# Fourteen weight pieces in turn behind the last transpose, and zero products counted by product time, in a one-core transformer block

## The chip, the core and the metric

The kernel runs on one core of a Trainium2 chip. The core has a matrix engine (PE, with its weight loads shown apart as PEld), a vector engine (DVE), a scalar engine (ACT), a general engine (POOL) and a sync engine (SP) that issues nearly all transfers. Every engine works through its own instruction queue strictly in order; engines wait for one another by semaphores. The metric is device time in microseconds (us), the median of several runs; lower is better.

## The reference, cut to what matters

One pre-norm transformer block on 2048 tokens of width 640: attention with 32 query heads of width 20 that share one key head and one value head, then a gated MLP of inner width 1536.

```python
n = layernorm(x)
q, k, v = n @ wq, n @ wk, n @ wv          # k and v have one head, q has 32
p = softmax(q k^T * 20 ** -0.5)           # every query sees all 2048 keys
h = x + (p @ v, heads side by side) @ wo
m = layernorm(h)
out = h + (gelu(m @ w_gate) * (m @ w_up)) @ w_down
```

## The kernel before

**Tiles and units.** The 2048 rows are 16 tiles of 128. Queries go in chunks of two tiles (the last two chunks have one). A unit is two groups of four heads for both tiles of a chunk (four groups where the chunk has one tile), which makes 512 columns in each of four row strips; a unit meets all 16 key tiles. One step, a unit with one key tile, is a *QK group*: four matmuls of 512 columns (L1149) that fill four score banks in PSUM. There are 512 QK groups in all. Scores are exponentiated either on ACT (L1489, into `pa`) or on DVE by an integer trick (L1583, into `pd`, copy 0); copies 1 and 2 of `pd` are copy 0 plus a constant, added on POOL (L1552, function `add_both`, both copies at once; L1538, one copy) or on DVE (L1532). *PV groups* (L1228) multiply `v_ext` with `pa` or `pd` into an accumulator bank. `v_ext` holds V times three factors; L604 makes the two scaled versions on POOL, 18 small instructions in the first 54 us.

**The head.** Each x tile is loaded, gets its statistics (L426), waits for a power on POOL (L446), is normed on DVE (L496, into `xn_tmp`) and transposed into `xn1T`: tiles 0 and 1 on PE, the other 14 by transposing transfers on SP (L487). When both tiles of a pair are in `xn1T`, a key/value job on PE (L548, reading `xn1T` and `wk`) makes their keys and values, copied out at L618 or L617. QK groups of the pair can follow only then.

**A finished unit.** Its accumulator is copied to `osb` on DVE (L1255), transposed by SP into `onr` (L725), and divided by its sums: a reciprocal on DVE (L679, waits for the transpose) and a product on POOL (L693). When a chunk is complete its rows are transposed (L754), multiplied with `wo`, normed again, and run through the MLP between the QK and PV groups of later chunks.

**What sets the order.** A planner in the kernel's Python builds all five queues before anything runs. It holds a modelled clock for each engine, takes the engine that is free first, and lets that engine's decision function commit the next instruction. Costs in the planner are constants: a QK or PV group 216 ns, a change between them 105 ns more (`pe_sw`), `add_both` 1010 ns, L604 100 ns for two tiles. Queues on the chip are then fixed in that order, whatever the chip's times turn out to be. So a changed cost or a moved transfer changes the order of later instructions all over the program.

**Weights.** Four loads on SP (L983) bring `wo` (800 KB), `wg`, `wu` and `wd` (1920 KB each). They may be planned once SP's modelled clock is past 30 us, with a lower priority than any transpose that is ready then.

**Zero products.** The clock of PE is granted by the chip and falls to half in some stretches. When PE has nothing else that fits, `fill` (L1352) adds a group of four matmuls with a zero weight into an open accumulator; the result is unchanged. `quiet` permits this when PE's planned busy time, changes of mode included, was under `QUIET` = 0.5 of the last 3400 ns. `fill` also asks that the unit has more than 8 products to come, and that the keys of tiles 0 to 3 are there.

Of the kernel before, what the change touches and what calls it, by code (L numbers as in the profile page):

```python
# [19 lines left out]


class _Op:
    __slots__ = ("eng", "fn", "deps", "t0", "end", "vis", "idx", "dma", "need", "count", "sem", "clock")

    def __init__(self, eng, fn, deps, t0, end, vis, dma):
        self.eng = eng
        self.fn = fn
        self.deps = deps
        self.t0 = t0
        self.end = end  # L30
        self.vis = vis
        self.dma = dma
        self.need = False
        self.count = 0
        self.sem = None
        self.clock = None


class _Plan:
# [60 lines left out]
    def resolve(self):  # L100


        pos = {e: 0 for e in self.ENGINES}
        known = {e: ({f: -1 for f in self.ENGINES}, set()) for e in self.ENGINES}
        self.waits = {e: [] for e in self.ENGINES}
        left = sum(len(v) for v in self.ops.values())
        while left:
            moved = False
            for e in self.ENGINES:
                while pos[e] < len(self.ops[e]):  # L110
                    op = self.ops[e][pos[e]]
                    if any(d.clock is None for d in op.deps):
                        break
                    kn, kd = known[e]
                    need = []
                    for d in sorted(op.deps, key=lambda o: -o.idx):
                        if (d in kd) if d.dma else (kn[d.eng] >= d.idx):
                            continue
                        need.append(d)
                        ck, cd = d.clock  # L120
                        for f in self.ENGINES:
                            kn[f] = max(kn[f], ck[f])
                        kd |= cd
                    best = {}
                    dmas = []
                    for d in need:
                        if d.dma:
                            dmas.append(d)
                        elif d.idx > best.get(d.eng, (-1, None))[0]:
                            best[d.eng] = (d.idx, d)  # L130

                    ws = sorted(dmas + [v[1] for v in best.values()], key=lambda d: d.vis)
                    for d in ws:
                        d.need = True
                    self.waits[e].append(ws)
                    ck = dict(kn)
                    cd = set(kd)
                    if op.dma:
                        cd.add(op)
                    else:  # L140
                        ck[e] = op.idx
                    op.clock = (ck, cd)
                    pos[e] += 1
                    left -= 1
                    moved = True
            assert moved, "the plan has a cycle"
        for e in self.ENGINES:
            n = 0
            for op in self.ops[e]:
                if op.need and not op.dma:  # L150
                    n += 1
                    op.count = n

    def emit(self, name, eng, sems):
        done = 0
        for op, waits in zip(self.ops[name], self.waits[name]):
            for d in waits:
                if d.dma:
                    eng.wait_ge(d.sem, 16)
                else:  # L160
                    eng.wait_ge(sems[d.eng], d.count)
            ins = op.fn(eng)
            if op.dma:
                ins.then_inc(op.sem, 16)
            elif op.need:
                ins.then_inc(sems[name], 1)
                done += 1
                assert done == op.count
# [36 lines left out]
def bass_sequential_preLN__grouped_kv_mqa__glu_gated_geglu__prompt_kernel(  # L205
# [126 lines left out]
        return n / 0.96 + 67.0  # L332

    POOL_ADD = 580.0
    POOL_ADD2 = 1010.0
    SP2 = 1
    SP2D = (450.0, 450.0, 450.0)
    SP2P = (3, 3, 3)
    SP2G = (300.0, 300.0, 300.0)
    ADD_MIN = 1  # L340
    PVF = 99
    QUIET = 0.5
    PADD_DVE = 1
    PADD_LEN = (3, 3, 3)
    PRA = 3
# [9 lines left out]
    LOCKW = 200.0  # L355
    YIELD = 500.0
    WQA = 1
    ADDW = 100.0
    MISCMAX = 1500.0
    L_PE, L_ACT, L_DVE, L_POOL = 232.0, 310.0, 150.0, 100.0  # L360
# [211 lines left out]
    def kv_job(tiles):  # L572
# [24 lines left out]
        def vthen(b):  # L597
            nt = len(tiles)
            vi = ps[:, b * 512:b * 512 + 32 * nt].rearrange("p (t e) -> p t e", t=nt)[:, :, 0:Dh]

            def vfin(op):
                free_bank(b)
                for w in (1, 2):
                    task(("pool",), (lambda w: lambda e: e.tensor_scalar(  # L604
                        v_ext[:, t0:t0 + nt, w, 0:Dh], v_ext[:, t0:t0 + nt, 0, 0:Dh], CH_W[w], None, ALU.mult))(w),
                        60 + 20 * nt, L_POOL, [("v", t, 0) for t in tiles] + [("vone", w)],
                        [("v", t, w) for t in tiles], 0)

            flex_copy(v_ext[:, t0:t0 + nt, 0, 0:Dh], vi, 20 * nt, [("b", b), ("vone", 0)],
                      [("v", t, 0) for t in tiles], 0.5, vfin)  # L610
# [157 lines left out]
    def wo_job(t, s, h):  # L768
        pieces = []
        for c in range(NC_D):  # L770
            pieces.append((mm(lambda b: bank(b, HALF), onT[:, s, c, :], wo_sb[:, c, h * HALF:(h + 1) * HALF],
                              c == 0, c == NC_D - 1), c_mm(HALF), [("onT", s), "wo"]))

        def then(b):
            if h == 1:
# [43 lines left out]
    def gu_pieces(w, b, fc):  # L819
        n = len(BATCHES[b]) * P  # L820
        x0 = xcol[BATCHES[b][0]]
        res = []
        for i in range(per_job(b)):
            f = fc + i
            for c in range(NC_D):
                res.append((mm((lambda i: lambda bk: ps[:, bk * 512 + i * n:bk * 512 + (i + 1) * n])(i),
                               w[:, c, f * P:(f + 1) * P], xn2T[:, c, x0:x0 + n], c == 0, c == NC_D - 1), c_mm(n),
                            [("xn2T", xcol[t]) for t in BATCHES[b]] + ["wg" if w is wg_sb else "wu"]))
        return res

    def gview(b, fc, k):
# [76 lines left out]
    def down_job(b, t, h):  # L908
        c0 = BATCH_COL[b] + (t - BATCHES[b][0]) * P
        pieces = [(mm(lambda bk: bank(bk, HALF), gbuf[:, fc, c0:c0 + P], wd_sb[:, fc, h * HALF:(h + 1) * HALF],  # L910
                      fc == 0, fc == NFC - 1), c_mm(HALF), [("g", fc, c0 // P), "wd"]) for fc in range(NFC)]

        def then(bk):
            down_left[b] -= 1
# [64 lines left out]
    for w in (1, 2):  # L979
        ptask((lambda w: lambda e: e.memset(shifts[:, w - 1:w], CH_SHIFT[w] * 65537))(w), 40, [],  # L980
              [("sh", w)], 1.5)
    for nm, o, v in (("wo", wo_sb, A_wo), ("wg", wg_sb, B_w_gate), ("wu", wu_sb, B_w_up), ("wd", wd_sb, B_w_down)):
        sp_tasks.append(_Task(("sp",), (lambda o, v: lambda e: e.dma_start(o[:], cview(v)))(o, v), 1500, 12000,  # L983
                              [], [nm], 9.0, None, lambda: plan.free["sp"] > 30000.0))

    def pe_sw(t, mode):

# [344 lines left out]
        return False  # L1332

    def quiet(t):
        busy = 0.0
        for o in reversed(plan.ops["pe"]):
            if o.end < t - 3400.0:
                break
            busy += min(o.end, t) - max(o.t0, t - 3400.0)
        return busy < QUIET * 3400.0  # L1340

    def fill(t):

        u = next((u for u in open_units() if u["acc"] is not None and all(u["started"]) and u["todo"] > 8), None)
        if u is None or not all(("k", k) in plan.w and plan.ready("pe", [("k", k)], ()) <= t for k in range(4)):
            return False
        ab = u["acc"]

        def fn(e):
            ins = None  # L1350
            for r in range(4):
                ins = e.matmul(ps[32 * r:32 * r + 32, ab * 512:(ab + 1) * 512], zz[:], kT4[:, 0:512], start=False,  # L1352
                               stop=False, tile_position=(0, 32 * r))
            return ins
        sw = pe_sw(t, "v")
        state["mode"] = "v"
        plan.commit("pe", fn, 216.0 + sw, L_PE, ["zz"] + [("k", k) for k in range(4)], [("b", ab)], at=t)
        state["fills"] = state.get("fills", 0) + 1
        return True

# [182 lines left out]

    def add_both(t):

        x = pend[1].pop(0)
        y = pend[2].pop(0)
        s = x["slot"]
        h = slice(s * 256, (s + 1) * 256)

        def fn(e):
            return e.tensor_tensor(pd32[:, 1:3, h], pd32[:, 0, h].unsqueeze(1).to_broadcast([P, 2, 256]),  # L1552
                                   shifts[:].unsqueeze(2).to_broadcast([P, 2, 256]), ALU.add)
        op = plan.commit("pool", fn, POOL_ADD2, L_POOL, [("pd", 0, s), ("sh", 1), ("sh", 2)],
                         [("pd", 1, s), ("pd", 2, s)], at=t)
        x["add"](1, op)
        y["add"](2, op)

    def dve_decide(t):
        imm = 1e12  # L1560
# [176 lines left out]
        return s  # L1737

    sems = {e: sem("c_" + e) for e in plan.ENGINES}
    n = 0  # L1740
    for e in plan.ENGINES:
        for op in plan.ops[e]:
            if op.dma:
                op.sem = sem("d%d" % n)
                n += 1
    outs = [op for op in plan.ops["sp"] if op.dma]

    with nc.Block() as block:

        @block.sync  # L1750
        def _(e):
            plan.emit("sp", e, sems)
            for op in outs[-NT:]:
                e.wait_ge(op.sem, 16)

        @block.scalar
        def _(e):
# [46 lines left out]
```

## Time and profile before

| | us |
|---|---|
| median of 5 runs | 793.57 |
| lowest and highest of them | 790.85, 795.47 |
| the profiled execution | 790.85 |
| span of the profiled execution, first to last instruction | 789.0 |
| ACT busy | 730.5 (93%) |
| PE busy (weight loads apart) | 694.2 (88%) |
| POOL busy | 655.6 (83%) |
| DVE busy | 614.0 (78%) |
| mean granted clock of PE | 0.984 |

The profile's page sums the whole program. Views of the trace go closer: the timeline lists instructions by start, with the idle time before each and what ended it; the chain follows the work that ended last back to its cause; a view by stretches gives for each one the busy time of an engine, the number of instructions in brackets, the granted PE clock, the busy share of the 16 transfer engines and the GB/s that they moved. "Issue to landing" is the time from the start of a transfer's instruction to the semaphore of its end. The program's zero products are 148 matmuls, so 37 groups.

### The profile page before, as it was taken

The numbers are of one execution on the slowest core, as the hardware profiler recorded it, in microseconds if no ns is written. First come the engines' busy times: TensorE is split into PE (matmuls) and PEld (weight loads), VectorE is DVE, ScalarE is ACT, GpSimd is POOL, SyncE is SP. The second block draws the span as 40 slices with busy tenths as digits, with TensorE's granted clock in tenths as the row PEclk, the third lists the DMA queues.
The fourth block names the chain that finished last, engine by engine and source line by source line (L and its number), as shares of the span: only waits on it lengthen the run. The fifth ranks groups of instructions, "written<-read, shape, count | busy, mean of one in ns | idle before, by whom it ended". The sixth has DMA issues, their size and how long they took to land.

```text
span 789.0 us, 29325 instructions
## 1 busy us (share of the span) xinstructions
PE 694.2 (88%) x12863; PEld 329.8 (42%) x12863; DVE 614.0 (78%) x1096; ACT 730.5 (93%) x1057; POOL 655.6 (83%) x708
## 2 busy tenths in 40 slices
PE   4768778897889899999888999999998889989998
PEld 3323223342234445445333444445444444434457
DVE  7938877888887887877888877868779787887854
ACT  5759999999999999999999999999999999999981
POOL 5559989899988998797997988788888898988860
PEclk9979999999999999999999999999999999999999
DMA  6790001100001002200011000110010000110000
GB/s 195 124 321 8 8 8 25 25 10 9 16 18 23 4 10 42 26 26 9 2 25 26 10 10 26 31 31 9 10 40 21 17 2 10 44 25 17 12 19 18
DMA packets 56606, 25.85 MB, mean 33 GB/s; under 512 B 47648, under 2 KB 55200, under 8 KB 56480
## 3 DMA queue, kind: packets, MB, share of 16 engines
q1 hardware_dynamic: 55168, 23.55, 13.3%
q8 instruction: 102, 1.67, 0.9%
q10 hardware_dynamic: 1312, 0.44, 0.2%
q14 instruction: 24, 0.20, 0.1%
HBM read 10.21 MB, written 2.62 MB: 16 GB/s over the span
## 4 chain that ended last, share of the span: by engine, by line
PE 56%; ACT 18%; DVE 17%; DMA 4%; POOL 3%; issue 2%; POOLq 0%
PE ps L548 21%; PE ps L1228 16%; PE ps L1149 16%; ACT pa L1489 14%; DVE pd L1583 11%; PE ps L544 3%; ACT gbuf L888 3%; POOL pd L1552 2%; DVE osb L1255 1%; DMA xn1T<-xn_tmp 1%; DVE xn_tmp L496 1%; DMA onT<-onq 1%; DMA xh<-in_A_x_dram 1%; ACT L1489 1%; ACT L888 1%
## 5 line engine op out<-in xcount | busy, mean ns | idle before, releaser
L1489 ACT ACTIVATE pa<-ps 128x512 bf16<-128x512 f32 (+1 forms) x1010 | 685.4, 823 | 30.7 <-PE ps L1149 25.3
L1552 POOL TENSOR_TENSOR pd<-pd,shifts 128x512 int32<-128x512 int32 x569 | 580.9, 1042 | 83.0 <-DVE pd L1583 78.2
L1583 DVE TENSOR_SCALAR pd<-ps 128x512 uint16<-128x512 f32 x621 | 415.9, 687 | 135.5 <-PE ps L1149 126.7
L1228 PE MATMUL ps<-pd,v_ext 128*32 128x512 bf16 x1863 | 289.2, 388 | 17.3 <-DVE osb L1255 10.3
L1228 PE MATMUL ps<-pa,v_ext 128*32 128x512 bf16 x1427 | 262.9, 390 | 3.7 <-ACT pa L1489 1.4
L1149 PE MATMUL ps<-qT,kT 32*128 32x512 bf16 x2048 | 204.9, 388 | 50.2 <-DVE pd L1583 32.7
L1149 PEld LDWEIGHTS ps<-qT,kT 32*128 32x128 bf16 x2048 | 56.8, 91 | 214.7 <-DVE pd L1583 131.4
L1228 PEld LDWEIGHTS ps<-pd,v_ext 128*32 128x32 bf16 x1863 | 80.0, 95 | 79.9 <-issue 35.5
L1228 PEld LDWEIGHTS ps<-pa,v_ext 128*32 128x32 bf16 x1427 | 71.0, 95 | 45.4 <-issue 27.0
L548 PE MATMUL ps<-xn2T,wu_sb 128*32 128x256 bf16 x1680 | 66.1, 274 | 2.8 <-DVE gbuf L905 1.7
L548 PE MATMUL ps<-xn2T,wg_sb 128*32 128x256 bf16 (+1 forms) x1748 | 67.4, 272 | 0.7 <-DVE gbuf L861 0.5
L548 PE MATMUL ps<-wd_sb,gbuf 128*32 128x320 bf16 x1344 | 65.3, 301 | 0.0
L548 PE MATMUL ps<-xn1T,wq_pad 128*32 128x256 bf16 (+1 forms) x1440 | 50.8, 267 | 0.8 <-POOL wq_pad L971 0.6
L548 PEld LDWEIGHTS ps<-xn2T,wg_sb 128*32 128x32 bf16 x1748 | 43.0, 96 | 19.7 <-issue 10.6
L548 PEld LDWEIGHTS ps<-xn2T,wu_sb 128*32 128x32 bf16 x1680 | 42.6, 96 | 19.7 <-issue 9.1
L548 PEld LDWEIGHTS ps<-wd_sb,gbuf 128*32 128x32 bf16 x1344 | 34.1, 96 | 24.1 <-issue 11.3
L548 PEld LDWEIGHTS ps<-xn1T,wq_pad 128*32 128x32 bf16 x1440 | 33.8, 98 | 14.3 <-issue 7.7
L905 DVE TENSOR_TENSOR gbuf<-ps,gbuf 128x512 bf16<-128x512 f32 x48 | 32.7, 682 | 8.5 <-PE ps L544 6.4
L1538 POOL TENSOR_TENSOR pd<-pd,shifts 128x256 int32<-128x256 int32 x50 | 33.5, 688 | 0.6 <-DVE pd L1583 0.6
L426 DVE BATCH_NORM_STATS2 stats<-xh 128x6 f32<-128x320 bf16 x64 | 29.9, 475 | 1.9 <-DMA xh<-in_A_x_dram 1.7
L548 PE MATMUL ps<-wo_sb,onT 128*32 128x320 bf16 x600 | 28.7, 301 | 0.8 <-DMA onT<-onq 0.7
L861 DVE CAST gbuf<-ps 128x512 bf16<-128x512 f32 x42 | 28.7, 683 | 0.9 <-PE ps L548 0.6
(73 smaller groups left out, 334.0 us busy)
## 6 DMA issues: line engine op xcount, KB each, us to landing
out_dram<-xh SPq DMA_DIRECT2D x16, 160.0 KB, 1.8
xh<-in_A_x_dram SPq DMA_DIRECT2D x3, 640.0 KB, 6.9
wg_sb<-in_B_w_gate_dram SPq DMA_DIRECT2D x1, 1920.0 KB, 10.9
wu_sb<-in_B_w_up_dram SPq DMA_DIRECT2D x1, 1920.0 KB, 10.7
wd_sb<-in_B_w_down_dram SPq DMA_DIRECT2D x1, 1920.0 KB, 15.4
wo_sb<-in_A_wo_dram SPq DMA_DIRECT2D x1, 800.0 KB, 5.2
onr<-osb SPq DMA_TRANSPOSE x30, 2.4
gbuf<-in_A_wq_dram ACTq DMA_DIRECT2D x1, 400.0 KB, 5.1
```

The costliest lines, as they stand in the source:

```text
L426: dve(lambda e: e.bn_stats(stats[:, ln, t, 6 * h:6 * h + 6], xh[:, t, h * HALF:(h + 1) * HALF]), 395, [key], [("st", ln, t, h)], prio, c)
L544: return e.matmul(o(b), l, r, start=st, stop=sp)
L548: ins = e.matmul(o(b)[a, :], l[:, a], r, start=st, stop=sp, tile_position=(0, 32 * j))
L861: dve(lambda e: e.tensor_copy(o, i), c_dve(n * k), [("b", bk)], ks, 1.0, fin)
L888: task(("act",), (lambda v: lambda e: e.activation(v, v, ACT.Gelu_apprx_tanh))(v), ("gelu", c_act(n * (f1 - f0))), L_ACT, ks, ks, 1.0, (la ...
L905: dve(lambda e: e.tensor_tensor(o, i, o, ALU.mult), c_dve(n * k), [("b", bk)] + ks, ks, 1.0, fin)
L1149: ins = e.matmul(bank(b), kT4[32 * r:32 * r + 32, kt * P:(kt + 1) * P], qT[32 * r:32 * r + 32, s, :], start=True, stop=True, tile_position ...
L1228: ins = e.matmul(ps[32 * r:32 * r + 32, ab * 512:(ab + 1) * 512], v_ext[:, it["kt"], it["w"], :], it["ap"], start=st, stop=(j in ends), ti ...
L1489: op = plan.commit("act", lambda e: e.activation(dst, src, ACT.Exp, scale=SM_SCALE), cost, L_ACT, [("b", b0 + i) for i in range(n)], [("pa ...
L1538: return e.tensor_tensor(pd32[:, w, h], pd32[:, 0, h], shifts[:, w - 1:w].to_broadcast([P, 256 * k]), ALU.add)
L1552: return e.tensor_tensor(pd32[:, 1:3, h], pd32[:, 0, h].unsqueeze(1).to_broadcast([P, 2, 256]), shifts[:].unsqueeze(2).to_broadcast([P, 2, ...
L1583: op = plan.commit("dve", lambda e: e.tensor_scalar(pd[:, 0, s * 512:(s + 1) * 512], bank(b), CH_A, CH_B, ALU.mult, ALU.add), c_dve(512), ...
```

## The change

**Weights.** Instead of four loads there are 14 pieces: `wo` in 2 (320 and 480 KB), `wg` and `wu` in 4 each (384, 384, 384 and 768 KB, since 5 row blocks are cut in 4), `wd` in 4 (480 KB each). The first piece may be planned when all 16 tiles of `xn1T` have their producer in the plan. Each further piece reads the key of the one before it, so SP waits on the chip for a piece to land before it issues the next. Costs in the planner: 560 ns on SP, landing 3000 ns (`W_LAT`) later. Matmuls that read a weight now wait for all its pieces.

**Semaphores.** Transfers that are known to be done before another is issued share a semaphore with it, which counts in steps of 16 (`chains`, `goal`).

**Zero products.** `QUIET` becomes 0.55; an instruction counts with at most 213 ns, so changes of mode no longer count as busy; `fill` needs more than 4 products to come (`FTODO`) instead of 8, and can use two key tiles (half as long a group) where four are not there yet.

**Costs in the planner.** L604 is planned with 180 + 75 ns per tile (330 for two) instead of 60 + 20 per tile; `add_both` may join up to `PBOTH` slots, which is 1, and costs 1000 ns instead of 1010.

```diff
@@ resolve
+        self.chains = []
+        for op in sorted((o for e in self.ENGINES for o in self.ops[e] if o.dma), key=lambda o: o.t0):
+            for c in self.chains:
+                if c[-1] in op.clock[1]:
+                    op.chain = c
+                    break
+            else:
+                op.chain = []
+                self.chains.append(op.chain)
+            op.chain.append(op)
+            op.goal = 16 * len(op.chain)
@@ constants
-    POOL_ADD2 = 1010.0
+    PBOTH = 1
-    QUIET = 0.5
+    QUIET = 0.55
+    FTODO = 4
+    W_LAT = 3000.0
@@ kv_job, scaled values on POOL
-                        60 + 20 * nt, L_POOL, [("v", t, 0) for t in tiles] + [("vone", w)],
+                        180 + 75 * nt, L_POOL, [("v", t, 0) for t in tiles] + [("vone", w)],
@@ weights
-    for nm, o, v in (("wo", wo_sb, A_wo), ("wg", wg_sb, B_w_gate), ("wu", wu_sb, B_w_up), ("wd", wd_sb, B_w_down)):
-        sp_tasks.append(_Task(("sp",), (lambda o, v: lambda e: e.dma_start(o[:], cview(v)))(o, v), 1500, 12000,
-                              [], [nm], 9.0, None, lambda: plan.free["sp"] > 30000.0))
+    w_pieces = []
+    for nm, o, v, n in (("wo", wo_sb, A_wo, 2), ("wg", wg_sb, B_w_gate, 4), ("wu", wu_sb, B_w_up, 4),
+                        ("wd", wd_sb, B_w_down, 4)):
+        rows = o.shape[1]
+        cut = [rows * i // n for i in range(n + 1)]
+        w_pieces += [(nm, i, o[:, x:y, :], cview(v)[:, x:y, :]) for i, (x, y) in enumerate(zip(cut, cut[1:]))]
+    W_KEYS = {nm: [(nm, i) for n2, i, _, _ in w_pieces if n2 == nm] for nm in ("wo", "wg", "wu", "wd")}
+    for k, (nm, i, o, v) in enumerate(w_pieces):
+        sp_tasks.append(_Task(("sp",), (lambda o, v: lambda e: e.dma_start(o, v))(o, v), 560, W_LAT,
+                              [w_pieces[k - 1][:2]] if k else [], [(nm, i)], 9.0 + 0.01 * k, None,
+                              (lambda k: lambda: all(("xn1T", t) in plan.w for t in range(NT)) and
+                               (k == 0 or w_pieces[k - 1][:2] in plan.w))(k)))
@@ quiet
-            busy += min(o.end, t) - max(o.t0, t - 3400.0)
+            busy += max(min(o.end, t) - max(o.end - min(o.end - o.t0, 213.0), t - 3400.0), 0.0)
@@ fill
-        u = next((u for u in open_units() if u["acc"] is not None and all(u["started"]) and u["todo"] > 8), None)
-        if u is None or not all(("k", k) in plan.w and plan.ready("pe", [("k", k)], ()) <= t for k in range(4)):
+        u = next((u for u in open_units() if u["acc"] is not None and all(u["started"]) and u["todo"] > FTODO), None)
+        n = 4 if all(("k", k) in plan.w and plan.ready("pe", [("k", k)], ()) <= t for k in range(4)) else 2
+        if u is None or not all(("k", k) in plan.w and plan.ready("pe", [("k", k)], ()) <= t for k in range(n)):
             return False
...
-        plan.commit("pe", fn, 216.0 + sw, L_PE, ["zz"] + [("k", k) for k in range(4)], [("b", ab)], at=t)
+        plan.commit("pe", fn, n * P / 2.4 + 3.0 + sw, L_PE, ["zz"] + [("k", k) for k in range(n)], [("b", ab)], at=t)
@@ add_both
-        op = plan.commit("pool", fn, POOL_ADD2, L_POOL, [("pd", 0, s), ("sh", 1), ("sh", 2)],
-                         [("pd", 1, s), ("pd", 2, s)], at=t)
+        op = plan.commit("pool", fn, 150.0 + 850.0 * k, L_POOL, [("pd", 0, i) for i in at] + [("sh", 1), ("sh", 2)],
+                         [("pd", w, i) for w in (1, 2) for i in at], at=t)
```

## The prediction

> **What bounds the kernel now.** I read the page first. ACT is busy 93% of the span, PE 88%, POOL 83%: no single engine is full over the whole, but ACT's row of slices reads 9 nearly throughout and 5, 7, 5 in the first three (0 to 59 us). So I asked for the head by stretches and chose three equal ones, the first beginning after the QK group at 42.8 us:
>
> ```profile
> 42.80:61.20 18.40, 11.94 (x120) 3.65 (x120) 6.19 (x11) 9.93 (x15) 9.71 (x12) 0.72 0.94 269
> 61.20:79.60 18.40, 15.50 (x236) 6.18 (x236) 15.06 (x25) 18.28 (x29) 17.63 (x20) 1.00 0.04 9
> 79.60:98.00 18.40, 14.56 (x209) 5.06 (x207) 15.34 (x25) 18.27 (x29) 17.79 (x21) 1.00 0.04 8
> ```
>
> The columns are PE, PEld, DVE, ACT, POOL, the granted clock, the share of the transfer engines and their GB/s. In the second and third stretch ACT is full (18.3 of 18.4 us). In the first it works 9.9 us, and everything else sags with it, while transfers are busy 94%. The same stretches for the QK groups alone (four matmuls each):
>
> ```profile
> 42.80:61.20 18.40, 3.60 (x28) 0.69 (x28) 0.72 0.94 269
> 61.20:79.60 18.40, 5.83 (x60) 1.74 (x60) 1.00 0.04 9
> 79.60:98.00 18.40, 5.61 (x60) 1.55 (x56) 1.00 0.04 8
> ```
>
> Seven groups where 15 fit. The chain of waits says what held them, and the timeline of SP says what stood in front of it:
>
> ```profile
> 38.94 0.09 ACT pa L1489
> 39.03 9.65 DMA xn1T<-xn_tmp
> 48.68 0.09 issue
> 48.77 1.26 PE ps L548 x16
> ```
>
> ```profile
> 35.11 0.77 SPq L983 DMA_DIRECT2D wo_sb<-in_A_wo_dram  x1
> 35.92 0.52 SPq L983 DMA_DIRECT2D wg_sb<-in_B_w_gate_dram  x1
> 37.26 5.78 SPq L487 DMA_TRANSPOSE xn1T<-xn_tmp  x2
> 43.08 0.58 SPq L983 DMA_DIRECT2D wu_sb<-in_B_w_up_dram  x1
> 43.70 2.85 SPq L983 DMA_DIRECT2D wd_sb<-in_B_w_down_dram  x1
> ```
>
> The last two transposes are issued 1.3 us and 3.1 us behind the `wg` load, which lands 10.9 us after its start, at 46.8. They land at 47.5 and 48.7, behind it. The spread of all 14 shows how unusual that is:
>
> ```profile
> L487 SPq DMA_TRANSPOSE xn1T<-xn_tmp x14: 1199/1279/4005, 13.1 to 39.0; - x14
> ...
> DMA to landing us min/median/max: 2.6/3.1/10.2
> ```
>
> After about 60 us the engines exchange the limit (the chain: PE 56%, ACT 18%, DVE 17%), with no wait longer than about 2 us. The stage the change aims at is thus 43 to 61 us.
>
> **Part 1: the weights leave the path of the last transposes.** With no load in front, the last transpose, issued at 39.03, lands after the median 3.1 us at 42.1 instead of 48.7. PE came to its key/value job at 43.5 (it idled 5.28 us before 48.77), so nothing waits any more. What is that worth? Below: PE's wait alone, 5.3 us. Above: the seven groups at the pace of 15 in 18.4 us need 8.6, so 18.4 - 8.6 = 9.8 us are lost. The larger figure has the second effect: behind the stall the clock was at one half from 47.6 to 57.8, and QK groups took 0.6 us instead of 0.4. The work of the last pair stays (a copy of 0.42 and one of 0.19 us on DVE, about 1 us of matmuls): I take 0.6 to 1.3 off and use **-8.5**. The queues are fixed, so all that follows moves forward with it, if its order were the same.
>
> **Part 2: the pieces on SP.** No row shows such a piece. Bounds: the first 160 KB loads of x took 2.7 us; at the 382 GB/s that the profile shows between 40 and 45 us the bytes are 0.43 of that, so 2.27 fixed. The 800 KB `wo` load took 5.2, which leaves 3.06 fixed, but it started behind two transposes that were to land 1.8 us later. Low: 14 x 2.27 + 6.72 MB / 382 GB/s = 31.8 + 17.6 = 49.4 us, 3.53 a piece. High: 14 x 3.06 + 17.6 = 60.4, or 4.32 a piece. I take the low one, since nothing runs in front of a piece. Here a rule speaks against the change: the Trainium skill, "DMA: Bandwidth & Descriptors", section "Rules for kernel authors", wants 1 MiB or more in a transfer, and its "Anatomy of one DMA" fits about 2.0 us plus bytes / 436 GB/s to each (measured there on the path that POOL issues). By that the pieces take 28 + 15.4 = 43.4 us (an estimate from the page); by the rows 49.4, against the 24 us that the four loads took (35.1 to 43.70 + 15.4 = 59.1). Both make loading slower, and neither charges the path: the first matmul with `wo` is at 131.3, with `wg` at 150.8, `wu` 261.4, `wd` 283.1, and the pieces, begun at 40.3, are in by about 90. Cover gone only if they took over 90 us.
>
> What can cost is the queue. SP now waits for each landing, and the transposes of finished units stand behind it (61.6, 81.1 and 102.0 before; about 53, 72 and 93 after). Behind them DVE's reciprocal (L679) and POOL's product (L693) wait in order, and behind those the exponentials on DVE. The planner spaces pieces by 560 + 3000 = 3.56 us. At 3.53 SP keeps up; at 4.32 it is 14 x 0.76 = 10.6 us late at the end, and the reciprocal has 0.9 us to spare (64.92 against 61.60 + 2.4). So 0 to +9.7; a piece in flight also delays a transpose by some of its own 1 to 2 us of streaming. I take **+0.5**. The 560 ns of issue on SP lie in SP's idle time.
>
> **Part 3: more zero products.** Two terms.
>
> The gain is the clock. Besides the stall there are three short drops in the steady part; one of them, with the stretch before:
>
> ```profile
> 98.78:102.19 3.41, 1.85 (x19) 0.60 (x21) 2.82 (x6) 3.38 (x6) 3.03 (x4) 1.00 0.00 0
> 102.19:105.61 3.42, 3.42 (x32) 0.73 (x24) 1.77 (x3) 2.52 (x5) 2.85 (x4) 0.50 0.28 43
> ```
>
> ACT loses 0.9 us in this one, 0.4 and 0.7 in those at 235 and 423; less the usual 0.1 each, 1.6 in all. The Trainium skill, "TensorE: Matmul & The Clock Gate", section "What's actually happening", has the clock fall after an idle stretch of some 3.4 us; by that none of the three would be touched, since PE was busy 1.8 us in each stretch before, and the term would be 0. The row disagrees: a half-empty stretch was enough. The measurement decides: in the stretches before the drops products fill 0.22 to 0.31 of the time (columns at 2.4 per ns over four concurrent tiles), and stretches at 0.35 to 0.38 kept the full clock, with one exception at 692 us. Filling towards 0.55 addresses that. I count half: **-0.8** (0 to -1.6).
>
> The price is PE time. Summing what the stretches between 61 and 430 us lack to 0.55, and dividing by 213 ns, gives about 70 groups more than the 37 of now; PE's own row for one is 0.22 us at full clock: 15.3 us of PE. They are planned where PE would idle, mostly waiting for score banks:
>
> ```profile
> PEld ps L1149 <- DVE pd L1583: 120.5, 333, 1.4
> PEld ps L1149 <- ACT pa L1489: 36.9, 58, 1.5
> ```
>
> That is 0.36 and 0.64 us per wait, longer than a group. Without that cover all 15 us count; I take a tenth, **+1.5** (0 to half, +7.7).
>
> **Part 4: costs and semaphores, one answer.** L604 really takes 309 ns, so its new price is nearer; no engine waited for it. `add_both` takes 1042 and is planned 10 ns shorter still; POOL is 17% idle. Shared semaphores do not change who waits. Together **0**. But the greedy order changes everywhere. A bound: five middle chunks do the same kind of work with 64 QK groups each and took
>
> ```profile
> 204.80:299.00 94.20, 25.95 (x256) 7.25 (x256) 0.98 0.09 17
> 299.00:389.00 90.00, 25.31 (x256) 7.03 (x256) 1.00 0.12 21
> 389.00:483.10 94.10, 25.75 (x256) 7.08 (x256) 0.98 0.08 17
> ```
>
> and 93.4 twice: a standard deviation of about 1.7 us each, so some 4 us over five of them, either sign.
>
> **Sum.** -8.5 + 0.5 - 0.8 + 1.5 + 0 = -7.3. The profiled execution goes from 789.0 to 781.7 of span, from 790.85 to 783.55 of time. It was the fastest of five, 2.72 below the median, so the median goes from 793.57 to **786.3**.
>
> **The rivals.**
>
> *The order falls well and the clock drops vanish.* The upper ends of part 1 and of the clock, -9.8 - 1.6, and 1 us of luck in the order: about 781. For it: the drops do cost ACT; against: nothing in the profile promises luck. Chance 0.18.
>
> *SP's queue becomes the wait (slower).* If a piece takes the 5.2 us of the `wo` row, SP falls 14 x 1.64 = 23 us behind by the third unit's transpose, and DVE stands 22 us in all at L679: 786.3 + 22 = 808. Slower than before by over 0.3% from 4.3 us a piece (14 x 0.76 less 0.9 eats the gain and 2.4 more). For it: the `wo` row; against: the 2.7 us of 160 KB. Chance 0.08.
>
> *Zero products on the path (slower).* PE has 56% of the chain; if all 70 groups delayed a QK group, +15.3 instead of +1.5 gives 800. It decides from 11.1 us, or 51 of the 70. Against: the waits above. Chance 0.08.
>
> *The stall stays.* If those transposes were slow for themselves, or their norm late, the time is 793.6. Against: the median of the 14 is 3.1 us, and 38.23 + 0.77 has the norm done at 39.0. Chance 0.06.
>
> **How the numbers follow.** The forecast's own case has 0.60, with 782 to 791 as its own range. About 0.3%, or 2.4 us, is what can be told from no change here: below 791.2 is faster, above 795.9 slower. Faster 0.60 + 0.18 = 0.78, same 0.06, slower 0.16. For 8 in 10 the range takes in the lucky case, 779, and the unchanged stall, 794; both slow cases and thin tails stay out.
>
> **What would show it.** Right: the last transposes land within 3.5 us; ACT has no idle time over 2 us between 40 and 60; the clock there is 1.0; 13 to 15 QK groups fit into 18.4 us from 42.8; pieces are about 3.5 us apart. Part 3: 90 to 120 zero groups, no more than one short drop after 60 us, QK waits not longer. Wrong: L679 or L693 waiting microseconds for `onr`, pieces over 4.3 us, a slower pace of QK groups between 100 and 700 us.

## The result, and the profile after

The changed kernel takes 788.19 us (786.1 to 791.35) where the kernel before took 793.12: ratio 0.9946, 95% interval 0.9933 to 0.9960, or about 4.3 us less (the two medians alone lie 4.9 apart). The forecast was 7.3 us less (786.3), in a range of 779 to 794. The direction was right, and the stall went as forecast; some 3 us are missing, and the runs below narrow down where they went.

The profiled execution has a span of 784.8 us. First the same three stretches of the head, of the changed kernel; the columns are PE, PEld, DVE, ACT, POOL, granted clock, share of the transfer engines, GB/s:

```profile
42.80:61.20 18.40, 15.62 (x243) 5.95 (x231) 12.11 (x21) 16.45 (x26) 15.89 (x20) 1.00 0.48 125
61.20:79.60 18.40, 15.36 (x219) 5.24 (x218) 15.30 (x25) 17.85 (x29) 17.91 (x20) 1.00 0.46 150
79.60:98.00 18.40, 15.87 (x226) 5.64 (x226) 15.39 (x25) 18.28 (x29) 17.04 (x21) 1.00 0.43 116
```

ACT works 16.5 us of the first stretch where it had worked 9.9, and the clock stays at 1.00 where it had been 0.72. The transfer engines, 94% busy before, are now under half busy in all three: the same bytes are spread out. The QK groups alone, in the same stretches:

```profile
42.80:61.20 18.40, 5.05 (x52) 1.45 (x52) 1.00 0.48 125
61.20:79.60 18.40, 5.63 (x60) 1.67 (x56) 1.00 0.46 150
79.60:98.00 18.40, 5.52 (x56) 1.52 (x56) 1.00 0.43 116
```

Thirteen groups instead of seven in the first. The timeline of SP and the chain of waits show the transposes clear of the loads, and the first unit's transpose between two pieces:

```profile
34.97 6.65 SPq L504 DMA_TRANSPOSE xn1T<-xn_tmp  x3
41.66 4.29 SPq L1009 DMA_DIRECT2D wo_sb<-in_A_wo_dram  x2
49.18 3.20 SPq L1009 DMA_DIRECT2D wg_sb<-in_B_w_gate_dram  x2
54.68 1.19 SPq L742 DMA_TRANSPOSE onr<-osb  x1
```

```profile
40.42 4.19 DMA xn1T<-xn_tmp
44.61 0.14 issue
44.74 0.73 PE ps L565 x20
```

The last transpose takes 4.19 us instead of 9.65. It lands at 44.61, not at the 42.1 of the forecast, and so misses the 3.5 us that were to show it right; the first piece went out 1.24 us behind it, and whether that slowed it is not shown. Next come the row of the zero products (its count is of matmuls, four to a group) and the wait at the reciprocal of a finished unit:

```profile
L1382 PE MATMUL ps<-kT,zz 128*32 128x512 bf16 x428 | 39.8, 398 | 0.0
```

```profile
DVE rcp L696 <- DMA onr<-osb: 0.3, 1, 0.3
```

There are 107 groups instead of 37; in the window from 60 to 110 us the reciprocal waited 0.3 us, once (1.7 us in three waits over the whole program). Apart from the head, one half-clock stretch is left (691.8 us).

How far ahead the changed kernel is can be read by setting the start of its k-th QK group against the same group of before: 6.9 us ahead at group 24, 8.9 at group 64, 7.9 at 192, 6.9 at 256, 5.6 at 448, and only 4.2 at the end of the span. These are two single executions, and the orders differ. Read so, the head won about what the forecast said, and the rest of the program gave about half of it back. Two questions followed: what is the head's gain made of, and who takes the rest: the zero products, the planner's costs, or the order?

### The profile page after: what moved, and what is told of

It reads as the page before. It is cut to its first block, busy times and chain, and to the rows that moved or that the text cites. A ratio compares the mean times of both kernels' runs of the same rounds, so it can differ in the third digit from the quotient of the medians.

```text
span 784.8 us, 29885 instructions
## 1 busy us (share of the span) xinstructions
PE 700.5 (89%) x13140; PEld 332.6 (42%) x13140; DVE 611.1 (78%) x1096; ACT 730.1 (93%) x1058; POOL 661.5 (84%) x713
## 4 chain that ended last, share of the span: by engine, by line
PE 54%; ACT 24%; DVE 16%; DMA 4%; issue 2%; POOL 1%
PE ps L565 20%; ACT pa L1519 19%; PE ps L1256 15%; PE ps L1177 15%; DVE pd L1620 9%; PE ps L561 3%; ACT gbuf L905 3%; DMA xn1T<-xn_tmp 2%; DVE osb L1283 1%; DVE xn_tmp L513 1%; PE ps L1382 1%; DMA onr<-osb 1%; DVE stats L443 1%; DMA xh<-in_A_x_dram 1%; ACT L1519 1%
## 5 line engine op out<-in xcount | busy, mean ns | idle before, releaser
L1586 POOL TENSOR_TENSOR pd<-pd,shifts 128x512 int32<-128x512 int32 x577 | 588.8, 1041 | 74.4 <-DVE pd L1620 69.5
L1256 PE MATMUL ps<-pd,v_ext 128*32 128x512 bf16 x1872 | 284.8, 383 | 18.2 <-DVE osb L1283 11.9
L1256 PE MATMUL ps<-pa,v_ext 128*32 128x512 bf16 x1424 | 256.5, 384 | 4.5 <-ACT pa L1519 2.1
L1256 PEld LDWEIGHTS ps<-pd,v_ext 128*32 128x32 bf16 x1872 | 78.4, 95 | 77.8 <-issue 32.3
L1382 PE MATMUL ps<-kT,zz 128*32 128x512 bf16 x428 | 39.8, 398 | 0.0
L1568 POOL TENSOR_TENSOR pd<-pd,shifts 128x256 int32<-128x256 int32 x47 | 31.6, 689 | 0.0
```

The lines of the kernel that those rows point to most:

```text
L1382: ins = e.matmul(ps[32 * r:32 * r + 32, ab * 512:ab * 512 + n * P], zz[:], kT4[:, 0:n * P], start=False, stop=False, tile_position=(0, 32 ...
L1568: return e.tensor_tensor(pd32[:, w, h], pd32[:, 0, h], shifts[:, w - 1:w].to_broadcast([P, 256 * k]), ALU.add)
```

## Experiments

Times are medians, with the ratio to runs of the kernel before made beside them (791.7 us in the first set, 792.5 in the second, 792.2 in the third). A bracket behind a ratio is its 95% interval, and "..." in a diff stands for lines left out. Two kinds of kernels are used. In some (x_...) the finished queues of a kernel are taken as they are and one thing is changed in them, so the order of all else stays. In the others the planner's inputs are changed and it orders everything anew.

### Whole loads behind the transposes, order kept

```diff
...
+    early = [o for o in q[:last] if o in (plan.w["wo"][0], plan.w["wg"][0])]
+    plan.ops["sp"] = [o for o in q[:last + 1] if o not in early] + early + q[last + 1:]
...
     plan.resolve()
```

> The kernel before with one thing moved: in SP's finished queue the wo and wg loads stand behind the last two transposes. All other queues are those of before, instruction for instruction. Theory (the stall behind the wg load is worth what QK groups lost there): the last transposes land within 4 us, no stall near 44 us, and everything after is the same order 6 to 9 us earlier: 784 to 787 us. Rival (the stall is made up later, so it was worth only PE's 5.3 us or less): 788 to 793.

Measured: 791.22 us, ratio 0.9992 (0.9975 to 1.001), so no gain that can be told from none. The theory's time was wrong, though its first half came true: the last two transposes land after 4.1 and 2.85 us, and at QK group 24 this kernel is 7.9 us ahead of before. At group 40 it is 2.5 ahead. (The profiled execution, 786.59 us, is the fastest of twelve. It ends 4.3 us ahead of the profiled one of before, so a lead late in this trace says nothing of the median; the loss between groups 24 and 40 is a step within one trace.) The chain of waits of this kernel shows what happened between:

```profile
53.23 0.60 DVE osb L1255
53.85 8.03 DMA onr<-osb
61.90 0.25 DVE rcp L679
62.15 0.56 DVE pd L1583
62.71 0.14 issue
62.84 0.61 PE ps L1149 x4
```

and its waits between 44 and 66 us (who waited for whom: us in total, times, longest):

```profile
PE ps L1149 <- DVE pd L1583: 5.9, 3, 4.9
...
DVE rcp L679 <- DMA onr<-osb: 4.8, 1, 4.8
POOL onq L693 <- DVE rcp L679: 4.7, 1, 4.7
```

All four loads are issued between 40.1 and 43 us and land until 61.5. The first unit's transpose, issued at 53.85, lands right behind them at 61.9. DVE stands at its reciprocal for 4.8 us, and the exponentials are queued behind that; PE waits, and its clock is at one half from 59.7 on for two stretches of 3.41 us. The stall has moved from one transpose to another. In the kernel before, the first unit's transpose was issued at 61.6, after the loads had landed (59.1), because the first stall had made it late.

### The 14 pieces, order kept

```diff
...
+    q = rest[:last + 1] + pieces[:4] + rest[last + 1:last + 2] + pieces[4:10] + rest[last + 2:last + 3] + pieces[10:] + rest[last + 3:]
+    plan.ops["sp"] = q
...
+    for e in plan.ENGINES:
+        for o in plan.ops[e]:
+            o.deps = [final.get(d, d) for d in o.deps]
     plan.resolve()
```

> The kernel before with its order kept on PE, DVE, ACT and POOL; on SP the four loads are replaced by the 14 chained pieces behind the last transpose, with the first unit's transpose after 4 pieces and the second after 10. Theory (whole loads moved behind the transposes only pass the stall on to the first unit's transpose, which landed after 8 us there; pieces leave it room): the 8 us that are won at 60 us stay, 783 to 785 against 791.7 before. Rival (the stall is made up later whatever the loads do): 788 or more, as with the whole loads moved.

Measured: 785.15 us, ratio 0.9907 (0.9875 to 0.9939), about 7.4 us less. PE, DVE, ACT and POOL run the very queues of before. The units' transposes in the window from 40 to 120 us, first with whole loads moved, then with pieces:

```profile
DMA to landing us min/median/max: 2.4/2.9/8.0
```

```profile
DMA to landing us min/median/max: 2.4/2.8/3.5
```

and DVE's wait for them with pieces:

```profile
DVE rcp L679 <- DMA onr<-osb: 0.3, 1, 0.3
```

It is 7.8 us ahead of before at group 64 and 7.1 at the end of the span. So the stall was worth about the price forecast, and it is not taken back later, if the loads leave room for the next small transfer. This is the cleanest measure of the weight part of the change, and it decides against the rival that the stall would be made up later. Two things stay untested: pieces left at the old place in front of the transposes, and pieces that do not wait for one another.

### No zero products, order kept

```diff
+    gone = {o for o in plan.ops["pe"] if getattr(o.fn, "__name__", "") == "fill_fn"}
+    plan.ops["pe"] = [o for o in plan.ops["pe"] if o not in gone]
...
     plan.resolve()
```

In the changed kernel:

> The changed kernel with its 107 groups of zero products taken out of PE's finished queue; nothing else moves, and the result is the same since they add zero. Theory (they pay: their clock is worth more than their PE time): the half-clock stretches come back, 789 to 793 us, slower than the changed kernel's 788.2. Rival (the 4 us that the changed kernel gives back after 200 us are zero products on PE's path): 783 to 786.

In the kernel before:

> The kernel before with its 37 groups of zero products taken out of PE's finished queue, order and result else the same. If zero products pay through the clock: more half-clock stretches, 795 to 799 us. If they only cost PE time: 790 to 792.

Measured: the changed kernel without its 107 groups takes 792.01 us, ratio 0.9999 (0.9976 to 1.0023), against 0.9946 with them: the groups are worth about 4.2 us, the time that they take on PE already paid. The kernel before without its 37 takes 795.35, ratio 1.0035 (1.0012 to 1.0059): they are worth about 2.8 us. Both times the rival (their PE time is what hurts) falls for this order. The mean granted clock of the executions goes from 0.994 to 0.978 in the one, from 0.980 to 0.967 in the other. One place where a drop came back, first the changed kernel, then the same order without zero products (columns as above):

```profile
691.00:694.50 3.50, 3.50 (x40) 0.81 (x36) 2.79 (x7) 3.03 (x5) 1.75 (x3) 0.61 0.34 68
695.10:701.90 6.80, 6.07 (x111) 2.66 (x111) 5.12 (x9) 6.60 (x11) 6.80 (x8) 0.99 0.13 27
```

```profile
691.00:694.50 3.50, 1.79 (x22) 0.51 (x22) 3.30 (x8) 3.04 (x6) 3.18 (x4) 1.00 0.00 0
695.10:701.90 6.80, 5.29 (x40) 1.21 (x40) 5.06 (x10) 5.57 (x8) 5.42 (x7) 0.50 0.31 60
```

After a stretch with PE busy 1.79 of 3.5 us, two stretches run at one half, and ACT does 5.57 us of work in 6.8 instead of 6.60.

What these two runs don't say is what the 70 groups that the new rule adds to the 37 are worth; they say what having none costs.

### Pieces alone, and with one further part each, ordered anew

The kernel before with the pieces of the change, old zero rule, old costs:

```diff
-    QUIET = 0.55
+    QUIET = 0.5
-            busy += max(min(o.end, t) - max(o.end - min(o.end - o.t0, 213.0), t - 3400.0), 0.0)
+            busy += min(o.end, t) - max(o.t0, t - 3400.0)
-                        180 + 75 * nt, L_POOL, [("v", t, 0) for t in tiles] + [("vone", w)],
+                        60 + 20 * nt, L_POOL, [("v", t, 0) for t in tiles] + [("vone", w)],
-        op = plan.commit("pool", fn, 150.0 + 850.0 * k, L_POOL, [("pd", 0, i) for i in at] + [("sh", 1), ("sh", 2)],
+        op = plan.commit("pool", fn, 160.0 + 850.0 * k, L_POOL, [("pd", 0, i) for i in at] + [("sh", 1), ("sh", 2)],
```

(the diff is against the changed kernel; `fill` is the old one too)

> The kernel before with the 14 pieces alone (gate, chain and W_LAT as in the change), old rule for zero products and old costs in the planner; the planner orders everything anew. Theory: the stall's 6 to 9 us, less up to 1 for waits on the pieces, plus or minus 4 for the new order: 782 to 790. Rival (SP's waits hold up DVE): over 791, with DVE waiting microseconds for onr.

Measured: 780.32 us, ratio 0.9852 (0.9827 to 0.9876): 7.4 us faster than the whole change by the ratios, and the fastest kernel here. The row of its zero products:

```profile
L1380 PE MATMUL ps<-kT,zz 128*32 128x512 bf16 x180 | 18.0, 383 | 0.0
```

Pieces with the new zero rule (only the two costs undone):

> Pieces and the new rule for zero products, old costs of L604 and the POOL addition in the planner. If the new rule's groups are what the changed kernel gives back against the pieces alone (780.3): 786 to 790. If the new costs are: 779 to 782. If it is only the luck of the new order: anywhere in 779 to 790.

Measured: 785.58, ratio 0.9920 (0.9893 to 0.9947). Pieces with the new costs (only the zero rule undone):

> Pieces and the new costs in the planner, old rule for zero products. If the new costs are what the changed kernel gives back: 786 to 790. If the new rule for zero products is: 779 to 782. If it is only the luck of the order: anywhere in 779 to 790.

Measured: 784.65, ratio 0.9903 (0.9871 to 0.9934). Neither part alone explains the 7.4 us, and both together (0.9946) are not clearly worse than either. That is what the luck of the order would look like, so the next kernels change nothing but the order.

### One nanosecond in the planner

The POOL addition's cost in the planner, 1 ns up or down. In the pieces alone:

```diff
-        op = plan.commit("pool", fn, 160.0 + 850.0 * k, L_POOL, [("pd", 0, i) for i in at] + [("sh", 1), ("sh", 2)],
+        op = plan.commit("pool", fn, 161.0 + 850.0 * k, L_POOL, [("pd", 0, i) for i in at] + [("sh", 1), ("sh", 2)],
```

> The pieces alone, with the planner's cost of the POOL addition 1011 instead of 1010 ns: a nanosecond that means nothing on the chip and still changes the order of thousands of rows. Theory (the order is luck of some 4 us either way): 3 us or more from the 780.3 of the pieces alone, most likely slower, 782 to 788. Rival (the order hardly matters, so differences between kernels have causes): 779 to 782.

Measured: 784.08, ratio 0.9898 (0.9869 to 0.9928), 3.6 us off by the ratios for one nanosecond. In the changed kernel (150.0 becomes 151.0, and 149.0):

> The changed kernel with the planner's cost of the POOL addition 1001 instead of 1000 ns. Theory (the changed kernel's 788.2 is an unlucky order of one and the same change): 781 to 787, so faster than it. Rival (pieces, zero rule and costs together cost those 4 us whatever the order): 787 to 790.

> The changed kernel with 999 instead of 1000 ns. Theory (luck of the order): 781 to 790, and some 2 us or more from the run with 1001 or from 788.2. Rival (a price of the change itself): 787 to 790, like its neighbours.

Measured: 787.13, ratio 0.9943 (0.9921 to 0.9964), and 785.27, ratio 0.9922 (0.9892 to 0.9952). In the kernel before (`POOL_ADD2` 1009 and 1011):

> The kernel before with 1009 instead of 1010 ns for the POOL addition. Theory (luck of the order of some 4 us either way, with the stall still in): 788 to 797, off from before by 2 us or more. Rival: within 1 us of before, 791 to 793.

> The kernel before with 1011 instead of 1010 ns. Theory: 788 to 797, off from before or from the run with 1009 by 2 us or more, and slower than every kernel that has the pieces by more than that on average. Rival: 791 to 793.

Measured: 798.26, ratio 1.0086 (1.0058 to 1.0114), and 789.82, ratio 0.9974 (0.9956 to 0.9991). Three plans of the kernel before that differ by a nanosecond lie 8.4 us apart.

| kernels (a nanosecond apart, or one part undone) | ratios to before | mean |
|---|---|---|
| before, 1009, 1011 | 1, 1.0086, 0.9974 | 1.0020 |
| pieces, old zero rule (f_w, f_w_1ns, f_wc) | 0.9852, 0.9898, 0.9903 | 0.9884 |
| pieces, new zero rule (changed kernel, a_1001, a_999, f_wz) | 0.9946, 0.9943, 0.9922, 0.9920 | 0.9933 |

The pieces show through all of it: in the table, every kernel that has them has a lower ratio than the fastest that has not (0.9946 against 0.9974, with intervals that just touch). They do not make up for everything: the changed kernel without zero products has the pieces too, and is no faster than before (0.9999). The expectation for the changed kernel's neighbours was half right: 999 is about 2 us faster by the ratios, 1001 is not. Whether the new zero rule costs something beside luck stays open. The ratios of its four kernels lie above the three with the old rule without overlap, 0.0049 or 3.9 us in the mean. Against a fixed cost stands that plans of before scatter by more than that. A reason can be argued, and is not shown: the fastest kernel has 45 zero groups and PE is busy with them for 18.0 us, the changed one has 107 and 39.8 us, at a mean clock of 0.994 in both. That pair flatters the old rule, though. Over all executions the mean clock is 0.987 to 0.994 in its three kernels and 0.994 to 0.997 in the four with the new rule, so the new rule's groups went with a somewhat higher clock and still with a longer time.

## Why the prediction was right, and where it was off

**The stall (part 1, -8.5) and the pieces (part 2, +0.5): right in sum, and in mechanism but for one step.** Together -8.0 was forecast; with the order kept they measure -7.4 (-9.9 to -4.8). Seven QK groups became 13, and the clock stayed up. But the step "with no load in front ... nothing waits any more" was half the story. It holds nearly for the last transposes (the last landed at 44.61, and PE waited 0.9 us for it, where it had waited 5.3). Whole loads moved behind them brought no gain clear of noise, because the next transpose in the queue takes over the stall. The prediction asked what the pieces' waits on SP could cost behind them, and not what they prevent: it credited the removal of the stall to the place of the loads, when the place alone is not enough. Its weighing of large against small transfers came out as said: the loading is longer, from 41.66 to 95.8 us, and no matmul waited for a weight.

**The size of a piece: near.** 14 pieces in 54.1 us, 3.87 each with two unit transposes between them, against 3.53 forecast, 3.56 in the planner and the 4.3 from which the second rival was to decide (its own terms, 14 x 0.76 less 0.9 against 7.8 + 2.4, give 4.35). The reciprocal of a finished unit hardly waited.

**The clock (part 3, gain -0.8): too small, by estimate.** Three drops were counted in one execution whose clock was 0.984. Over the 29 executions of before in the first set the mean is 0.980, and the time goes with it: 3.8 us per 0.01 of mean clock (correlation -0.74; the other two sets give 5.3 and 4.7). One half-clock stretch of 3.41 us is 0.5 x 3.41 / 789 = 0.0022 of the mean, so it costs about 0.8 us. From 0.980 to 0.994 are some 6 stretches, 5 us. Three of the six are the stall's own and were counted there, which leaves about 2.5 us. The term was mis-sized because the profiled execution had fewer drops than most. Its reading of how full a stretch must be is only a rough one too: counted anew from the same trace, the stretches before the three drops are filled to 0.23, 0.32 and 0.33, and the exception at 692 us is one at 0.21 that kept the clock. In the kernel with the moved loads one at 0.32 kept it as well (from 203 us), so these traces show a tendency and no threshold.

**The price of zero products (+1.5): not seen by itself.** With the order kept, taking them out made both kernels slower, so their gain is larger than their price; the price alone was not measured. The forecast of 90 to 120 groups (107) and of at most one drop after 60 us was met.

**The order (part 4, 0 with 4 either way): where the missing 3 us went, most likely.** It was left at zero, with a bound read from the scatter of equal chunks. From the pieces in before's order, 0.9907, to the changed kernel, 0.9946, the sum moves 3.1 us the wrong way, although its zero products pay. A nanosecond moved such kernels by 0.2 to 6.8 us, so this size needs no cause; a cost of the new zero rule of up to some 4 us can't be told from it. The bound of 4 us was somewhat small (6.8 us once), and the sum had no way to know the sign. That the time fell within a few us of the forecast is thus partly luck: the same change with one nanosecond less in the plan takes 785.27 us.

**Rivals.** The lucky order (0.18) exists: it is the pieces alone at 780.3, not the change as made. SP's queue as the wait and a stall that stays are ruled out for the changed kernel by the rows above. Zero products on the path as a net loss are ruled out against having none, and not against having the 37 of the old rule.

## What to carry to other kernels

Here small transfers that were issued behind bulk loads landed only with the loads, so look for the next small transfer in the queue before moving a load behind the present one; chained pieces that left gaps freed both transposes, the moved loads only one. When queues come from a greedy planner, compare changes in a fixed order, or over several neighbouring plans: here one nanosecond of planned cost could move the time by as much as the change did. Judge what a clock drop costs by the clock of many executions, not of the one in the profile.

## What was not expected of the hardware

One program's executions spread over 787 to 796 us, and the time often goes with the mean granted clock: 3.8 us per 0.01 in the kernel before, correlations of -0.85 (loads moved) and -0.90 (changed kernel without zero products), but hardly any in two others (-0.07 with pieces and the new zero rule, -0.12 in the kernel before with 1009). The drops within these programs come in stretches of 3.41 us and multiples of it (6.83 and 10.24). A transpose behind bulk loads on the same queue landed with the last of them: 61.88 against 61.46 us for the `wd` load that was issued 12 us earlier.
